# Transposing e by DMA in fours instead of pairs, in the backward pass of grouped-query attention

## The chip, the cores and the metric

The kernel runs on one core of a Trainium2 chip. The metric is the device time of one execution in microseconds (us), and the number of record is the median over runs of the kernel on the chip. A profiled execution is one more run, with its own time. The engines are named PE (TensorE, matmuls), PEld (its weight loads), DVE (VectorE), ACT (ScalarE), POOL (GpSimd) and SP (SyncE, which here only issues DMAs).

## What is computed

The reference is the forward and the backward pass of two attention blocks whose outputs stand side by side. Block A is linear attention; the kernel does it first, before the stage described below, and the change doesn't touch it. Block B, which the change is about, is softmax attention with 16 query heads that share one key and one value head (S = 2048 tokens, D = 448, head size 28):

```
q = x @ wq ; k = x @ wk ; v = x @ wv
p = softmax(q k^T * 28**-0.5) ; o = p v          # per head
B = o (heads side by side) @ wo
outputs: concat([A, B], -1) and the gradients of all eight inputs and weights, given grad_out
```

For the backward pass the kernel needs, for each head, do = grad_out @ wo^T, dV = p^T do, dS = p * (do v^T - rowsum(do * o)), dQ = dS k and dK = dS^T q.

## The kernel before

After block A and the projections of block B, one long stage (from about 229 us on, here called the core) does attention and its gradient together. Its work is cut into 64 **blocks** b of 256 queries x 2 heads (8 query chunks qc, 8 pairs of heads), and each block into 8 **units** of 256 keys; u = 8b + tp counts the 512 units. The loop over u (28 more steps run it dry) is written out by hand under a manual schedule: the order in the source is the order on each engine. In the step of unit u:

- `rows_SD` (L625 by its helper `mmt`) puts the scores of unit u into PSUM banks sps (matmuls with 32 rows of the array), and for unit w = u - 16 the products do v^T into banks dps.
- ACT takes the exponential e of each head's scores into an SBUF slot **eT** (L861 and L899, 128 x 512 each). A slot of eT holds two units (4 KB per partition); ten slots rotate.
- For unit w = u - 16, DVE multiplies dps of one head by e (L866), ACT copies that of the other to SBUF (L868, cp), POOL multiplies it (L869); the results are dsT. DVE transposes dsT in 32 x 32 squares for dK (L931).
- In odd units, when a slot is full, SP issues one DMA that transposes it whole, 128 x 2048 values of 2 bytes, 512 KB, into a slot of **eN** (L902). Twelve slots of 4 KB rotate, and a block has four.
- PE adds e v to oq for the two units before (`o_mm`), dS k for units 18 to 20 back (`dq_mm`), in odd units dK for blocks 27 units behind (`dk_m`), and in even units one **quarter** of dV (`dv_mm`): four matmuls of 512 columns, one per eN slot of the block, in the order c = 0 to 3. dV's quarters of block b are at u = 8b + 18, 20, 22 and 24.
- `due(u, lag)` is the block whose first unit lies lag units back. With it, once per block, DVE copies o^T from oq (lag 9), PE turns it (`onat_T`, lag 10), DVE and POOL normalise it (`o_norm`, lag 10) into the rows do_nat, where it takes the place of do; and so on up to lag 27, where dQ is stored.

Two kinds of work are laid between the units in a spare PSUM bank, at most one per unit: `do_proj`, 32 halves of do for the 16 row tiles (its slots are in the dictionary do_slots), and `out_proj`, the output o @ wo in halves (`out_part` says which half at which unit; four of each query chunk's after it is done, at 64(q+1) + 24 to + 48, and the last two tiles whole at u = 532 and 536). Its left operand, o transposed, is made by an SP transpose of 256 KB after every 8 blocks (L891, into oTq), which stands in the same queue as those of e.

From u = 512 on `post_load` brings grad_out (L711), x (L716) and weights into freed slots of eT and eN through SP's queue, in even units, and from u = 519 `gwo` computes the gradient of wo from them. Then the last stage computes dx, dwk, dwv and dwq.

SP takes its DMAs strictly in order: each waits for its own data, and those behind it wait too.

Of the kernel before, what the change touches and what calls it, by code (L numbers as in the profile page):

```python
# [9 lines left out]
ALU = mybir.AluOpType  # L10
# [14 lines left out]
def kernel(  # L25
# [580 lines left out]
    with ExitStack() as cs_:  # L606
        psA = psc.enter_context(tc.tile_pool(name="psAcc", bufs=1, space=bass.MemoryType.PSUM))
        pe_ = cs_.enter_context(tc.tile_pool(name="ceT", bufs=10, side="right"))
        pn_ = cs_.enter_context(tc.tile_pool(name="ceN", bufs=12, side="right"))
        pd_ = cs_.enter_context(tc.tile_pool(name="cdsT", bufs=5, side="right"))  # L610
# [10 lines left out]

        eT, eN, dsT, dsx, qX, don, doT, rl, prod = ({} for _ in range(9))

# [37 lines left out]
        wo = pp_.tile([P, 4, D], BF16, name="wo", bufs=1)  # L661
        oTq = {}

        def out_part(u):
            n, q_ = (u % 64 - 24) // 8, u // 64 - 1
            if u >= NU and u in (532, 536):
                n = (u - 532) // 4
            elif q_ < 0 or n not in (0, 1, 2, 3) or u % 8 or u >= NU:
                return None
            return (2 * q_ + n, 0, D) if u >= NU else (2 * q_ + n // 2, n % 2 * (D // 2), (n % 2 + 1) * (D // 2))  # L670

        ots = {}

        def out_proj(i, c0, c1, ps):
            for c in range(4):
                mm(ps[:, 0:c1 - c0], oTq[i // 2][:, 4 * (i % 2) + c, :], wo[:, c, c0:c1], start=(c == 0), stop=(c == 3))

# [7 lines left out]
        def by_tokens(t):  # L685
            return t.rearrange("p (t d) -> p t d", d=512)
# [8 lines left out]
        def post_load(k):  # L695
            if k == 4:
                post["dkvT"], mix = (pn_.tile([P, 16, P], BF16, name="eN").rearrange("p a b -> p (a b)") for _ in range(2))
                post["dkvn"], post["wkvT"] = mix[:, 0:1024], mix[:, 1024:1024 + D]
                zero(post["wkvT"][64:128, :])
                nc.sync.dma_start(post["wkvT"][0:64, :], wkvT_d[:, :])  # L700
            if 5 <= k < 9:
                zero(post["dkvT"][64:128, 512 * k - 2560:512 * k - 2048])
            i = k % 4
            rows = slice(i * 512, (i + 1) * 512)
            if k == 8:
                t = pe_.tile([P, 2, 2, 512], BF16, name="eT").rearrange("p a b c -> p (a b c)")
                post["wqT"] = t[:, 0:4 * D].rearrange("p (g c) -> p g c", c=D)
                nc.sync.dma_start(post["wqT"], wqT_d[:, :].rearrange("(g p) c -> p g c", p=P))
            elif k < 4:
                t = by_tokens(pe_.tile([P, 2, 2, 512], BF16, name="eT").rearrange("p a b c -> p (a b c)"))  # L710
                nc.sync.dma_start(t[:, :, 0:D], go2[rows, D:2 * D].rearrange("(t p) d -> p t d", p=P))  # L711
                post["gb"] += [t[:, j, :] for j in range(4)]
            else:
                t = by_tokens(pe_.tile([P, 2, 2, 512], BF16, name="eT").rearrange("p a b c -> p (a b c)"))
                zero(t[:, :, D:512])
                nc.sync.dma_start(t[:, :, 0:D], Bx2[rows, :].rearrange("(t p) d -> p t d", p=P))  # L716
                post["xb"] += [t[:, j, :] for j in range(4)]
# [76 lines left out]
        def o_mm(v):  # L794
            b, tp = divmod(v, 8)
            for t2 in range(2):
                t = 2 * tp + t2
                for h in range(2):
                    mmt(oq[32 * h:32 * h + 32, 0:256], vaug[:, t, :],
                        eT[v // 2][:, v % 2, h, t2 * 256:(t2 + 1) * 256], (0, 32 * h), t == 0, t == 15)  # L800
                yield
# [17 lines left out]
        def dv_mm(b, h, qb):  # L819
            for c in range(4):  # L820
                rhs = eN[4 * b + c][:, :, :].rearrange("p (u h t q) k -> p u h t q k", u=2, h=2,
                                                       t=2)[:, :, h, :, qb, :]
                mmt(dv_acc[32 * c:32 * c + 32, :], don[b][:, qb, h, :], rhs, (0, 32 * c),
                    b == 0 and h + qb == 0, b == NB - 1 and h + qb == 2)
# [5 lines left out]
        def do_copy(i, h, ps):  # L830
            nc.vector.tensor_copy(out=do_nat[:, i, h * 256:(h + 1) * 256], in_=ps[:, 0:256])

        free = [*range(1, 16), *range(17, 27, 2), *range(32, 64, 8),
                *[64 * q_ + i for q_ in range(1, 6) for i in (0, 8, 16, 56)]]
        do_slots = {u: divmod(n, 2) for n, u in enumerate(free[0:2 * NS])}
        with tc.manual_schedule():
            tc.keep_in_program_order(nc.scalar.activation(out=ex[:], in_=ex[:], func=ACT.Exp))
            for u in range(NU + 28):
# [18 lines left out]
                if hasS:  # L857
                    if u % 2 == 0:
                        eT[u // 2] = pe_.tile([P, 2, 2, 512], BF16, name="eT")
                    et = eT[u // 2]  # L860
                    nc.scalar.activation(out=et[:, u % 2, 0, :], in_=sp[0][:, :], func=ACT.Exp, scale=scale)  # L861
                if hasD:
                    dst = pd_.tile([P, 2, 512], BF16, name="dsT")
                    dsT[w] = dst
                    ew = eT[w // 2]
                    nc.vector.tensor_tensor(out=dst[:, 0, :], in0=dp[0][:, :], in1=ew[:, w % 2, 0, :], op=ALU.mult)  # L866
                    cp = pc_.tile([P, 512], BF16, name="cp")
                    nc.scalar.activation(out=cp[:, :], in_=dp[1][:, :], func=ACT.Copy)  # L868
                    nc.gpsimd.tensor_tensor(out=dst[:, 1, :], in0=cp[:, :], in1=ew[:, w % 2, 1, :], op=ALU.mult)  # L869
                for a in {10: (0, 2), 18: (1, 3)}.get(u, ()) or {38: (0, 2), 54: (1, 3)}.get(u % 64, ()) * (u < 448):  # L870
# [15 lines left out]
                if (b := due(u, 10)) is not None:  # L886
                    o_norm(b)
                    if b % 8 == 7:
                        q_ = b // 8
                        oTq[q_] = pp_.tile([P, 8, P], BF16, name="oTq", bufs=1)  # L890
                        nc.sync.dma_start_transpose(oTq[q_][:, :, :], do_nat[:, 2 * q_:2 * q_ + 2, :].rearrange("p q c -> p (q c)"))  # L891
                if (b := due(u, 14)) is not None:
# [5 lines left out]
                if hasS:  # L898
                    nc.scalar.activation(out=et[:, u % 2, 1, :], in_=sp[1][:, :], func=ACT.Exp, scale=scale)  # L899
                    if u % 2 == 1:  # L900
                        en = pn_.tile([P, 16, P], BF16, name="eN")
                        nc.sync.dma_start_transpose(en[:, :, :], et[:, :, :, :].rearrange("p a b c -> p (a b c)"))  # L902
                        eN[u // 2] = en

# [5 lines left out]
                else:  # L910
                    o_dq((u - 2, u - 1), (u - 20, u - 19))
                    b, n = divmod(u - 18, 8)
                    if 0 <= b < NB:
# [121 lines left out]
```

## Time and profile before

| | |
|---|---|
| median of 5 runs | 1106.34 us |
| the runs | 1110.08, 1105.51, 1099.61, 1112.46, 1106.34 us |
| the profiled execution, its own time | 1108.78 us |
| its span (first to last instruction) | 1107.1 us |
| mean granted TensorE clock | 0.994 |
| the core: first exponential L899 to the last one | 229.5 to 1025.8 us |
| first and last dV matmul | 255.1 and 1056.1 us |

The span is counted from the first instruction of the program on the core; all times of the profile are from there. Where a row gives three numbers with slashes they are the least, the median and the greatest duration in ns; "x256" is a count; "out<-in" names what an instruction writes and reads. In brackets stands the idle time of the engine before the instruction and what ended it. In a row of SP, the duration is how long the issue held SP, not how long the transfer took.

### The profile page before, as it was taken

The page shows a single profiled execution, that of the slowest core. Times are in us where ns is not written, and L with a number is a line of the kernel's source. Part 1 is how long each engine was busy: PE and PEld are TensorE (multiplying, and loading weights), DVE is VectorE, ACT ScalarE, POOL GpSimd, SP SyncE. Part 2 cuts the span into 40 slices and gives each one's busy share as a digit, 9 for nine tenths or more (in the row PEclk, how much of TensorE's full clock was granted, in tenths as well). Part 3 has the DMA queues.
Part 4 walks back from the last instruction along what each step waited for, and adds up shares of the span by engine and source line. Part 5 has one row for each costly group of instructions (what it writes and reads, how often), then busy time and mean ns, then how long its engine had stood idle before and what let it go on. Part 6 is the DMA issues. An engine that isn't in the chain of part 4 may idle for free.

```text
span 1107.1 us, 39142 instructions
## 1 busy us (share of the span) xinstructions
PE 1050.2 (95%) x15640; PEld 490.4 (44%) x15645; DVE 897.4 (81%) x1772; ACT 875.9 (79%) x1744; POOL 757.9 (68%) x986
## 2 busy tenths in 40 slices
PE   9999999988999999999999999989999999999998
PEld 5545555444444444444444434434444444444344
DVE  7887400438999999999999999989999999999742
ACT  6453122568999999999999999989999999999421
POOL 6001242227888888889888988978988898888640
PEclk9999999999999999999999999999999999999999
DMA  9869899099999999999999999999999999999962
GB/s 264 149 124 178 174 189 221 27 202 185 203 183 183 187 185 184 181 193 182 190 182 191 192 186 181 189 177 188 191 191 195 182 185 188 195 183 191 218 138 63
DMA packets 672534, 199.01 MB, mean 180 GB/s; under 512 B 649584, under 2 KB 668320, under 8 KB 672352
## 3 DMA queue, kind: packets, MB, share of 16 engines
q1 hardware_dynamic: 660512, 175.19, 99.2%
q0 software_dynamic: 6880, 17.37, 6.5%
q10 hardware_dynamic: 4960, 3.96, 1.2%
q8 instruction: 122, 2.00, 0.7%
q14 instruction: 60, 0.49, 0.1%
HBM read 21.00 MB, written 12.94 MB: 31 GB/s over the span
## 4 chain that ended last, share of the span: by engine, by line
PE 52%; DVE 27%; DMA 7%; ACT 7%; issue 6%; POOL 0%; SPq 0%; DVEq 0%; ACTq 0%
PE agen L80 13%; PE dk_acc L625 11%; DVE dsx L931 10%; DVE dsT L866 9%; DMA eN<-eT 5%; PE sps L80 5%; PE oq L625 5%; ACT eT L899 5%; PE aacc L80 4%; PE sps L625 4%; PE dps L625 4%; PE dv_acc L625 2%; DVE R L884 2%; DVE oTs L881 2%; DVE oTs L754 1%
## 5 line engine op out<-in xcount | busy, mean ns | idle before, releaser
L869 POOL TENSOR_TENSOR dsT<-cp,eT 128x512 bf16<-128x512 bf16 x512 | 588.3, 1155 | 120.0 <-ACT cp L868 108.9
L866 DVE TENSOR_TENSOR dsT<-dps,eT 128x512 bf16<-128x512 f32 x512 | 342.8, 669 | 31.0 <-PE dps L625 23.6
L931 DVE STREAM_TRANSPOSE dsx<-dsT 128x512 f32<-128x512 f32 x512 | 357.5, 698 | 2.0
L861 ACT ACTIVATE eT<-sps 128x512 bf16<-128x512 f32 x512 | 313.0, 611 | 38.2 <-PE dps L625 25.4
L625 PEld LDWEIGHTS <-R 32*128 32x128 bf16 (+1 forms) x8192 | 203.5, 94 | 295.7 <-issue 268.3
L868 ACT ACTIVATE cp<-dps 128x512 bf16<-128x512 f32 x512 | 314.2, 614 | 14.6 <-PE dps L625 13.3
L899 ACT ACTIVATE eT<-sps 128x512 bf16<-128x512 f32 x512 | 320.8, 627 | 0.0
L625 PE MATMUL dk_acc<-dsx,qX 32*32 32x512 bf16 x4096 | 268.8, 377 | 0.0
L625 PE MATMUL dps<-doT,R 32*128 32x256 bf16 x2048 | 249.7, 270 | 12.5 <-DVE dsT L866 7.3
L625 PE MATMUL sps<-R,R 32*128 32x256 bf16 x2048 | 217.8, 274 | 3.7 <-DVE oTs L754 2.0
L625 PE MATMUL oq<-eT,R 128*32 128x256 bf16 x2048 | 158.6, 276 | 0.0
L625 PE MATMUL oq<-dsT,R 128*32 128x256 bf16 x2048 | 158.4, 276 | 0.1
L625 PEld LDWEIGHTS <-qX 32*32 32x32 bf16 x4096 | 79.9, 89 | 114.9 <-issue 54.8
L625 PE MATMUL dv_acc<-eN,don 128*32 128x512 bf16 x1024 | 112.4, 381 | 9.6 <-DMA eN<-eT 9.6
L80 PEld LDWEIGHTS <-R 128*128 128x128 bf16 (+1 forms) x553 | 45.8, 99 | 47.8 <-issue 20.3
L396 POOL MEMSET ga<- 64x448 bf16 x2 | 0.9, 470 | 95.1 <-DVE pr L347 81.8
L546 DVE TENSOR_TENSOR osb<-R 32x512 bf16<-32x512 bf16 x4 | 1.7, 414 | 62.1 <-ACT R L543 62.1
L625 PEld LDWEIGHTS <-don 128*32 128x32 bf16 x1024 | 33.9, 98 | 0.6
L80 PE MATMUL agen<-R,R 128*128 128x448 bf16 x128 | 28.6, 353 | 0.9 <-ACT R L219 0.6
L874 POOL DMA_DIRECT2D qX<-qn_d x32 | 18.1, 570 | 16.2 <-DMA qn_d<-gaT 16.2
L884 DVE TENSOR_SCALAR R<-oq 64x256 bf16<-64x256 f32 x64 | 27.3, 427 | 2.0
L744 PE MATMUL sps<-identF,oTs 64*128 64x64 f32 x128 | 21.4, 247 | 7.4
(220 smaller groups left out, 1010.8 us busy)
## 6 DMA issues: line engine op xcount, KB each, us to landing
qX<-qn_d POOLq DMA_DIRECT2D x32, 256.0 KB, 6.3
eN<-eT SPq DMA_TRANSPOSE x256
out_dram<-osb ACTq DMA_DIRECT2D x22, 112.0 KB
qn_d<-gaT SPq DMA_DIRECT2D x2, 1024.0 KB
xa<-in_A_x_dram SPq DMA_DIRECT2D x8, 224.0 KB
ga<-in_grad_out_dram SPq DMA_DIRECT2D x4, 448.0 KB
xa<-in_grad_out_dram POOLq DMA_DIRECT2D x4, 448.0 KB, 5.7
out_dram<-wdq POOLq DMA_DIRECT2D x8, 224.0 KB, 4.0
```

Of the source, the lines that this page charges most:

```text
L80: nc.tensor.matmul(out_ap, lhsT=lhsT, rhs=rhs, start=start, stop=stop, tile_position=(0, 0))
L625: nc.tensor.matmul(out, lhsT=lhsT, rhs=rhs, start=start, stop=stop, tile_position=pos, skip_group_check=True)
L744: nc.tensor.transpose(onp[:, qb, :, :].rearrange("p h c -> p (h c)"), oTs[0:64, qb * P:(qb + 1) * P], identF[0:64, 0:64], tile_position=(0 ...
L861: nc.scalar.activation(out=et[:, u % 2, 0, :], in_=sp[0][:, :], func=ACT.Exp, scale=scale)
L866: nc.vector.tensor_tensor(out=dst[:, 0, :], in0=dp[0][:, :], in1=ew[:, w % 2, 0, :], op=ALU.mult)
L868: nc.scalar.activation(out=cp[:, :], in_=dp[1][:, :], func=ACT.Copy)
L869: nc.gpsimd.tensor_tensor(out=dst[:, 1, :], in0=cp[:, :], in1=ew[:, w % 2, 1, :], op=ALU.mult)
L874: nc.gpsimd.dma_start(qX[qc][32 * a:32 * a + 32, :, :, :].rearrange("j b s c -> j b (s c)"), qn_d[qc * 256:(qc + 1) * 256, :].rearrange("( ...
L881: nc.vector.tensor_copy(out=oTs[0:64, :], in_=oq[0:64, 0:256])
L884: nc.vector.tensor_scalar(out=qT_B[g][64 * hp:64 * hp + 64, qc * 256:(qc + 1) * 256], in0=oq[64:128, 0:256], scalar1=scale, scalar2=None, ...
L899: nc.scalar.activation(out=et[:, u % 2, 1, :], in_=sp[1][:, :], func=ACT.Exp, scale=scale)
L931: nc.vector.transpose(out=dsx[b][:, tp, :, :, :].rearrange("p h t c -> p (h t c)").bitcast(F32), in_=dsT[y][:, :, :].rearrange("p h c -> p ...
```

## The change

- eT becomes five fixed tiles of four units (8 KB per partition), eN six fixed tiles of 32 x 128 values; both take as much memory as before. `eT(u)` and `eN(b, c)` name the parts. Tiles are no longer taken from a rotating pool, so each reader and writer is ordered by the part of the tile that it touches.
- SP's transpose is issued once per four units, when u % 4 is 3: 128 x 4096 values, 1 MB.
- dV's quarters move two units back: u = 8b + 20, 22, 24 and 26.
- o is transposed after blocks 15, 31 and 47 for two query chunks at once (512 KB), and after 55 and 63 for one; the target is R4, which held the weights of do_proj before. For that, all do_proj slots now lie before u = 128 (the last at 120 instead of 184), and the halves of out_proj lie 16 units apart at 144 to 256 and 272 to 384, and 8 apart at 400 to 456 and 464 to 488.
- The loads after u = 512 go into parts of the same fixed tiles.

The lines of the code shift by a few: L861, L866, L868, L869, L899 and L902 become L865, L870, L872, L873, L903 and L905, and L891 becomes L894.

```diff
-        pe_ = cs_.enter_context(tc.tile_pool(name="ceT", bufs=10, side="right"))
-        pn_ = cs_.enter_context(tc.tile_pool(name="ceN", bufs=12, side="right"))
+        pe_ = cs_.enter_context(tc.tile_pool(name="ceT", bufs=1, side="right"))
+        pn_ = cs_.enter_context(tc.tile_pool(name="ceN", bufs=1, side="right"))
...
+        ETs = [pe_.tile([P, 4, 2, 512], BF16, name=f"eT{i}") for i in range(5)]
+        ENs = [pn_.tile([P, 32, P], BF16, name=f"eN{i}") for i in range(6)]
+
+        def eT(u):
+            return ETs[u // 4 % 5][:, u % 4, :, :]
+
+        def eN(b, c):
+            return ENs[(2 * b + c // 2) % 6][:, 16 * (c % 2):16 * (c % 2) + 16, :]
...
-        oTq = {}
+        oTq = flat(R4).rearrange("p (t k) -> p t k", k=P)
+        outs = {128 * m + 144 + 16 * n: 8 * m + n for m in range(2) for n in range(8)}
+        outs.update({400 + 8 * n: 16 + n for n in range(8)})
+        outs.update({464 + 8 * n: 24 + n for n in range(4)})
...
         def post_load(k):
...
+            t = ETs[(128 + k // 2) % 5][:, 2 * (k % 2):2 * (k % 2) + 2, :, :].rearrange("p a b c -> p (a b c)")
...
-        free = [*range(1, 16), *range(17, 27, 2), *range(32, 64, 8),
-                *[64 * q_ + i for q_ in range(1, 6) for i in (0, 8, 16, 56)]]
-        do_slots = {u: divmod(n, 2) for n, u in enumerate(free[0:2 * NS])}
+        do_slots = {u: divmod(n, 2) for n, u in enumerate([*range(1, 16), *range(17, 27, 2), *range(32, 128, 8)])}
...
-                    if b % 8 == 7:
-                        q_ = b // 8
-                        oTq[q_] = pp_.tile([P, 8, P], BF16, name="oTq", bufs=1)
-                        nc.sync.dma_start_transpose(oTq[q_][:, :, :], do_nat[:, 2 * q_:2 * q_ + 2, :].rearrange("p q c -> p (q c)"))
+                    if b in (15, 31, 47, 55, 63):
+                        t0, t1 = 2 * (b // 8) - 2 * (b < 48), 2 * (b // 8) + 2
+                        nc.sync.dma_start_transpose(oTq[:, 4 * (t0 % 4):4 * (t0 % 4) + 4 * (t1 - t0), :],
+                                                    do_nat[:, t0:t1, :].rearrange("p q c -> p (q c)"))
...
-                    if u % 2 == 1:
-                        en = pn_.tile([P, 16, P], BF16, name="eN")
-                        nc.sync.dma_start_transpose(en[:, :, :], et[:, :, :, :].rearrange("p a b c -> p (a b c)"))
-                        eN[u // 2] = en
+                    if u % 4 == 3:
+                        nc.sync.dma_start_transpose(ENs[u // 4 % 6][:, :, :],
+                                                    ETs[u // 4 % 5][:, :, :, :].rearrange("p a b c -> p (a b c)"))
...
-                    b, n = divmod(u - 18, 8)
+                    b, n = divmod(u - 20, 8)
                     if 0 <= b < NB:
                         dv_mm(b, n // 4, n // 2 % 2)
```

## The prediction

> **What bounds the kernel now.** I read the page first, for where the time lies.
>
> ```profile
> span 1107.1 us, 39142 instructions
> ...
> PE   1050.2 (95%) x15640; PEld 490.4 (44%) x15645; DVE 897.4 (81%) x1772; ACT 875.9 (79%) x1744; POOL 757.9 (68%) x986
> ...
> DMA  9869899099999999999999999999999999999962
> ...
> q1 hardware_dynamic: 660512, 175.19, 99.2%
> ...
> PE 52%; DVE 27%; DMA 7%; ACT 7%; issue 6%; POOL 0%; SPq 0%; DVEq 0%; ACTq 0%
> ```
>
> The stage that the change touches runs from about 229 us (first exponential) to 1056 us (last dV matmul), and its 512 units are nearly all of it. Four engines are at nine tenths or more there, so nothing that shortens one engine's work alone pays much. Beside them stands SP's DMA queue, q1, busy throughout, and the chain passes through a DMA for 7%. So the next view is that of the tile eN: what is issued into it, and who waits for it.
>
> ```profile
> L902 SPq DMA_TRANSPOSE eN<-eT x256: 1334/2982/7247, 235.8 to 1030.0; - x128
> ...
>   DMA eN<-eT: 9.6, 8
> ```
>
> 256 issues in 235.8 to 1030.0 is one per 3.11 us, and an issue holds SP for 2.98 us in the median: SP hardly rests. The waits view books some 700 us of SP's waiting at L902 to ACT, and that is misleading. The timelines show it:
>
> ```profile
> 641.16 0.60 ACT L899 ACTIVATE eT<-sps 128x512 bf16<-128x512 f32 x1
> ```
> ```profile
> 645.43 1.25 SPq L891 DMA_TRANSPOSE oTq<-R  x1
> 646.79 18.51 SPq L902 DMA_TRANSPOSE eN<-eT  x7
> ```
> ```profile
> 652.34 0.42 PE dk_acc L625 x5
> 652.76 6.13 DMA eN<-eT
> 658.89 0.04 issue
> 658.93 0.38 PE dv_acc L625
> ```
>
> The exponential at 641.16 (unit 263) ends at 641.76, and its pair is issued only at 652.76, 11.0 us later, behind earlier pairs. It lands at 658.89, 17.1 us after its data was ready, just too late for dV, whose first quarter reads it 11 units after that exponential: 11 x 1.54 = 16.9 us (a block of 8 units takes 12.33 us by the starts of L899, 12.0 where it has no projection of do or out). Over the run a pair lands 14.6 us after its exponentials in the median and 17.7 in the worst twentieth. Thus the transposes form a queue that is exactly as fast as the engines: 4 x 3.11 = 12.4 us per block, against 12.0 to 12.33. It drifts into the deadline, stops PE, and drifts off. All eight stops lie at the first quarter's fourth chunk, so at one place of the block.
>
> **What a stop costs.** The eight make 9.6 us of idle PE (2.02, 0.50, 0.38, 0.83, 1.42, 0.95, 2.48, 1.05). Refilling costs about 0.3 more each: across the stop of 1.42, L899 starts 3.46 us after the one before, where the same place of undisturbed blocks has 1.70, so 1.76 in all. That is 2.4. And the two longest cost the clock:
>
> ```profile
> 735.49 0.38 PE L625 MATMUL dv_acc<-eN,don 128*32 128x512 bf16 x1 [2.48 <-DMA eN<-eT]
> ```
> ```profile
> 736.15:739.56 3.41, 3.41 (x48) 1.17 (x44) 2.76 (x6) 2.50 (x5) 1.15 (x1) 0.50 0.97 184
> 740.00:750.00 10.00, 9.65 (x186) 4.15 (x178) 9.47 (x19) 9.93 (x21) 8.20 (x9) 1.00 1.20 194
> ```
>
> The columns are the window, its length, each engine's busy time with its count, the granted clock and DMA. 48 matmuls in 3.41 us, where the next stretch does 18.6 per us: (63 - 48) / 18.6 = 0.8 us lost, and by the same count 1.2 at 258.3 to 261.7. Here the row differs from a rule. The Trainium skill ("TensorE: Matmul & The Clock Gate", Part 1) has the clock drop after at least one idle window of about 3.4 us. By it these stops, all under 2.5 us, keep the clock, and eight cost 9.6 + 2.4 = 12.0. By the trace, stops of 2.02 and 2.48 did lose it and one of 1.42 did not, and the cost is 12.0 + 2.0 = 14.0. I take the trace. Adding up instead how much longer the nine disturbed units are gives 13.4; I use that.
>
> **The change, part by part.**
> *Four units per transpose.* It removes 128 of 256 issues; bytes and 256 B packets stay. What an issue costs by itself is read from small ones:
>
> ```profile
> L103 SPq DMA_TRANSPOSE wvT<-R x4: 1192/1242/1356, 26.8 to 30.8; - x4
> ```
> ```profile
> L891 SPq DMA_TRANSPOSE oTq<-R x8: 1247/1250/1420, 345.8 to 1034.3; - x8
> ```
>
> 128 KB take 1.24 us, 256 KB 1.25, 512 KB (eN) 1.33 at the least: a floor of 1.2 us whatever the size. So 128 x 1.2 = 154 us of SP's time go; SP's time is not the path, the stream's is. Upper bound of the gain in the stream: the whole floor, 1.2 us per quad. Lower bound: nothing, since in most of the trace's packets one transpose follows the other with no gap. In the few cycles with no other queue's packet near, packets nearly cease for 0.5 us at the seam of two transposes. Here a rule speaks against the change: the skill ("DMA: Bandwidth & Descriptors", Anatomy of one DMA) says that the fixed part of a DMA is dominated by completion latency, not setup, and with a second transpose already issued that is hidden. By it the gain is 0. The rows of 1.24 us against 1.33 show setup, on the issuing side. I take 0.3 us per quad, nearer to the packets than to the floor: 6.2 - 0.3 = 5.9 us per quad, against 6.0 to 6.17 us in which the engines make one. A loss can't be excluded, as no row has a transpose of 1 MB; I keep 0.3 us the other way as that end.
>
> *dV two units later.* Its first quarter now comes 13 units after its last exponential, 20.0 us instead of 16.9. A quad hands over its first pair 3.1 us later than before; with a queue at work this moves nothing, as the bytes ahead are the same, and without a queue a quad lands after some 1.3 + 2 x 1.9 + 1.5 = 7 us. So 3 us of slack come with it. I set the 256 measured landing-to-landing intervals against block periods free of stops. With no gain in the stream quads still stop PE for some 5 us, since arriving in lumps eats the slack; with 0.25 us per quad no stop is left after the first block; with 0.5 us of loss PE stops in half the blocks.
>
> *Waits.* The exponential of unit 4k+20 now waits for a quad issued after unit 4k+3, 16 units before: 24.7 us, later than dV's 20.0, so dV is hit first. Behind it on ACT stand cp and the other exponential, thus everything, if it were late. POOL's and DVE's reads of the same slot lie four units back, as before three. A quad's own target is freed by dV at unit 8b+26 and the quad comes at 8b+27, as 8b+24 and 8b+25 before: nothing.
>
> *o, out and do.* Eight transposes of 256 KB become three of 512 and two of 256: 3 x 1.25 us of SP, hidden as above. The halves of out_proj (28) and the do_proj slots (32) keep their number and stay one per block at a unit divisible by 8, beside the 0.36 us that each costs a block today (12.33 - 12.0). dV's quarters stay one per even unit. All at nothing; if two fell into one block, 0.36 us each.
>
> *The end.* SP issues the last pair near 1030 and the first load of grad_out after it at 1033.68; PE waits for that load:
>
> ```profile
> 1038.96 0.54 PE L80 MATMUL sps<-eT,R 128*128 128x448 bf16 x2 [1.71 <-DMA eT<-in_grad_out_dram]
> ```
>
> and is at half clock at 1040.0 to 1043.3. With a queue that has drained, the last quad (ready at 1026.4) would be issued by 1027 and leave SP at 1031, so the load comes some 2 us earlier: 1.7 + 1 at best, 0 if the queue is as long as now. I take 1.5.
>
> **Sum**, against the profiled execution's 1108.8 us: 13.4 in the units, less 1 for a stop in the first blocks, where the queue starts 12 us late behind the q transposes, and 1.5 at the end: 1108.8 - 12.4 - 1.5 = 1094.9. The profiled execution lies 2.4 above the median of 1106.3, and stops vary from run to run (1099.6 to 1112.5), while a drained queue has none; so I leave it at **1094.5**, 1.07% under the median. Nothing more can come: the engines' own 12.0 to 12.33 us per block stay.
>
> **Rivals.**
> *The stream gains nothing* (setup is hidden already). For it: packets that abut in most of the trace, q1 at 99%. Then slack and lumps cancel, 5 of the 9.6 us stay, and the time is 1106.3 - 4 = 1102, between 1099 and 1109.
> *A 1 MB transpose is slower than two halves* (slower end). Place: every seam of the queue; the point from which it decides is 6.17 us per quad, today's 2 x 3.11 being at the edge. At 0.3 us over, 128 x 0.3 = 38 us, less the slack of 3, plus clock losses: about 1140. For it: service varies widely already (1.3 to 7.2 us) and no row has the size. Against: same bytes, same packets.
> *The engines are the bound anyway* and stops hide other work: against it, L899's periods lengthen by the full stop each time.
>
> **From cases to numbers.** Drained queue 0.56 (1088 to 1099), no gain 0.28 (1099 to 1109), slower transposes 0.16 (1109 to 1150). A measurement of this kernel tells about 1% from no change, that is 1095.3 to 1117.4. The first case straddles the lower bound: faster 0.44, same 0.43, slower 0.13. The range of 8 in 10 leaves out 0.05 below and 0.14 above: **1088 to 1113**; the likeliest case alone 1088 to 1099.
>
> **What would show it.** Right: eN's 128 issues with a median near 5.5 us, but gaps between them, no wait of dv_acc for eN after the first block, no half-clock window inside the units, blocks still at 12.0 to 12.33 us, the first grad_out load before 1033. No gain: issues back to back at 6.1 us and two to five stops, now at units 8b+20. Wrong: issues over 6.2 us and dv_acc waiting in most blocks, or ACT's exponentials waiting for the eT slot.

## The result, and the profile after

| | before | after |
|---|---|---|
| median of all runs | 1108.89 us (73 runs) | 1097.2 us (38 runs) |
| range | 1096.1 to 1123.3 us | 1094.8 to 1102.7 us |
| ratio, 95% interval | | 0.9918, 0.9903 to 0.9932 |
| profiled execution, its span | 1108.78, 1107.1 us | 1097.16, 1095.4 us |
| first exponential of the core, start | 229.5 us | 230.2 us |
| last one, start | 1025.8 us | 1016.9 us |
| from there to the end of the span | 81.3 us | 78.5 us |

By the ratio the change saves 0.8%; the ratio compares fast runs alone, those within 1.5% of the fastest of their kernel, and so leaves out the longest ones of before, while the medians of all runs lie 1.05% apart. The spread of the runs shrinks from 27 to 8 us. That this is because PE's stops varied from run to run is inferred: each kernel has one profile. The page of the changed kernel first, in the lines that answer to those shown of before:

```profile
span 1095.4 us, 38646 instructions
...
PE 1045.2 (95%) x15640; PEld 490.6 (45%) x15645; DVE 895.9 (82%) x1772; ACT 875.7 (80%) x1744; POOL 757.2 (69%) x986
...
DMA  9879899199999999999999999999999999999962
...
q1 hardware_dynamic: 656320, 175.18, 92.9%
...
PE 34%; POOL 25%; ACT 23%; issue 11%; DVE 4%; DMA 2%; SPq 0%; POOLq 0%; ACTq 0%; DVEq 0%
...
L633 PE MATMUL dv_acc<-eN,don 128*32 128x512 bf16 x1024 | 108.7, 379 | 0.0
```

The engines do the same work as before. What has changed is q1: 92.9% of the span instead of 99.2% for the same 175 MB, so the queue now rests. The idle time ahead of dV's matmuls (the last column, 9.6 us before) is 0.0, and DMA has fallen from 7% to 2% of the chain that ended last. That chain now runs more through POOL and ACT (25% and 23%) than through PE and DVE as before; no run here tests which engine sets the length of a block. The view of the tile eN:

```profile
L905 SPq DMA_TRANSPOSE eN<-eT x128: 4699/5326/7697, 236.4 to 1017.5; - x128
```

The median hold is 5.33 us. From the first issue to the last it is 781 us, 6.15 us from issue to issue, which the engines set now: SP's holds sum to 682 us, and between its DMAs it rests for 93 us in all, where it rested for 28 before. 101 of the 128 quads go out within 0.1 us of the end of their last exponential, where pairs went out 3 to 13 us late. The longest delays follow a 512 KB transpose of o:

```profile
430.99 5.37 SPq L905 DMA_TRANSPOSE eN<-eT  x1
...
437.08 3.10 SPq L894 DMA_TRANSPOSE R<-R  x1
...
440.29 10.51 SPq L905 DMA_TRANSPOSE eN<-eT  x2
```

The timeline puts the quad of 440.29 behind o's 3.10 us; it is 3.4 us late, and the lateness has drained two to three blocks on. In the middle of the core blocks take 11.97 and 12.39 us by turns, like the undisturbed blocks of before.

The start of the core got worse. The timeline of 236 to 249 us after:

```profile
236.36 4.97 SPq L905 DMA_TRANSPOSE eN<-eT  x1
...
241.50 0.46 SPq L580 DMA_DIRECT2D qn_d<-gaT  x1
...
247.45 0.18 DVE L762 RECIPROCAL rl<-sps 128x4 f32<-128x4 f32 x1 [4.69 <-DMA qn_d<-gaT]
247.67 0.29 DVE L763 TENSOR_TENSOR oTs<-sps,rl 128x128 f32<-128x128 f32 x1
...
248.01 0.39 PE L633 MATMUL sps<-R,R 32*128 32x256 bf16 x4 [3.66 <-DVE oTs L763]
```

The same place before, by its chain of waits:

```profile
235.84 2.12 SPq L902
...
238.13 6.11 DMA qn_d<-gaT
```

And the matmul that waited there, by the timeline of before:

```profile
244.93 0.39 PE L625 MATMUL sps<-R,R 32*128 32x256 bf16 x4 [1.19 <-DVE oTs L754]
```

On SP the first transpose of e stands ahead of the second store of q to DRAM (L580). A pair held SP for 2.12 us, a quad for 4.97, so the store goes out at 241.50 instead of 238.13. DVE's reciprocal rl (one over the row sums of the softmax) has nothing to do with q, but its tile was given memory from which that store still reads; so it waits 4.69 us, and PE waits 3.66 us for what DVE makes of it (1.19 before). The granted clock falls to half from 248.6 to 252.0. That it is the memory was read from the kernel here; a run further down moves the tile.

At the other end the first load of grad_out goes out 5.5 us after the start of the last exponential, 7.9 before; PE doesn't wait for it any more, and no window of half clock is left there:

```profile
1005.58 16.68 SPq L905 DMA_TRANSPOSE eN<-eT  x3
...
1022.37 0.55 SPq L720 DMA_DIRECT2D eT<-in_grad_out_dram  x1
```

### The profile page after: what moved, and what is told of

Its sections match the earlier page's. It is cut to its first block, busy times and chain, and to the rows that moved or that the text cites. A ratio compares the mean times of both kernels' runs of the same rounds, so it can differ in the third digit from the quotient of the medians.

```text
span 1095.4 us, 38646 instructions
## 1 busy us (share of the span) xinstructions
PE 1045.2 (95%) x15640; PEld 490.6 (45%) x15645; DVE 895.9 (82%) x1772; ACT 875.7 (80%) x1744; POOL 757.2 (69%) x986
## 3 DMA queue, kind: packets, MB, share of 16 engines
q1 hardware_dynamic: 656320, 175.18, 92.9%
## 4 chain that ended last, share of the span: by engine, by line
PE 34%; POOL 25%; ACT 23%; issue 11%; DVE 4%; DMA 2%; SPq 0%; POOLq 0%; ACTq 0%; DVEq 0%
POOL dsT L873 22%; ACT cp L872 13%; PE agen L80 12%; ACT eT L903 9%; PE aacc L80 4%; PE sps L80 4%; PE oq L633 4%; PE sps L633 2%; PE dv_acc L633 2%; PE dps L80 1%; DVE dsx L934 1%; PE dps L633 1%; PE dk_acc L633 1%; POOL prod L767 1%; POOL don L770 1%
## 5 line engine op out<-in xcount | busy, mean ns | idle before, releaser
L873 POOL TENSOR_TENSOR dsT<-cp,eT 128x512 bf16<-128x512 bf16 x512 | 587.7, 1155 | 105.7 <-ACT cp L872 97.5
L870 DVE TENSOR_TENSOR dsT<-dps,eT 128x512 bf16<-128x512 f32 x512 | 342.4, 669 | 16.3 <-PE dps L633 9.1
L865 ACT ACTIVATE eT<-sps 128x512 bf16<-128x512 f32 x512 | 313.0, 611 | 28.8 <-PE dps L633 12.5
L872 ACT ACTIVATE cp<-dps 128x512 bf16<-128x512 f32 x512 | 315.1, 615 | 11.6 <-PE dps L633 8.0
L903 ACT ACTIVATE eT<-sps 128x512 bf16<-128x512 f32 x512 | 321.6, 628 | 0.0
L633 PE MATMUL dv_acc<-eN,don 128*32 128x512 bf16 x1024 | 108.7, 379 | 0.0
L80 PEld LDWEIGHTS <-R 128*128 128x128 bf16 (+1 forms) x673 | 57.1, 98 | 55.1 <-issue 24.6
L499 ACT ACTIVATE wdq<-agen 128x448 bf16<-128x448 f32 x16 | 8.7, 542 | 25.3 <-PE agen L80 25.3
```

The lines of the kernel that those rows point to most:

```text
L80: nc.tensor.matmul(out_ap, lhsT=lhsT, rhs=rhs, start=start, stop=stop, tile_position=(0, 0))
L633: nc.tensor.matmul(out, lhsT=lhsT, rhs=rhs, start=start, stop=stop, tile_position=pos, skip_group_check=True)
L865: nc.scalar.activation(out=eT(u)[:, 0, :], in_=sp[0][:, :], func=ACT.Exp, scale=scale)
L903: nc.scalar.activation(out=eT(u)[:, 1, :], in_=sp[1][:, :], func=ACT.Exp, scale=scale)
```

## The experiments

My theory was that the size of the transposes does it: fewer issues, a shorter stream, so the queue drains. Rivals: the later deadline of dV does it; or the fixed tiles and the rarer transposes of o. Four kernels take the change apart. Ratios are to the kernel before.

**Quads, but dV at its old place.** The changed kernel with

```diff
-                    b, n = divmod(u - 20, 8)
+                    b, n = divmod(u - 18, 8)
```

> The changed kernel with dV's quarters back at 8b+18 to 8b+24: quads, fixed tiles and the new o transposes stay, the later deadline goes. Issue theory (each transpose costs the queue about 0.9 us beside its bytes, so half as many make the queue faster than the engines and it runs empty): a quad lands some 7 us after its last exponential, far before the 16.4 us at which dV comes, so no wait of dV for eN and the time of the changed kernel, 1096 to 1098 us. Slack theory (the two units are what removes the stops): stops come back, 1102 to 1109 us, with dV waiting for eN in several blocks.

Measured: 1098.16 us, ratio 0.9925 (0.9896 to 0.9954). By its profile no dV matmul waits for eN; eN's row is as after:

```profile
L905 SPq DMA_TRANSPOSE eN<-eT x128: 4709/5258/7664, 235.5 to 1017.1; - x128
```

So the two units of slack aren't needed: a quad that is issued in time, with the queue at rest, lands 6.3 us after its issue in the median.

**Each quad as two halves, issued one after the other.** The changed kernel; bytes, tiles, deadline and unit stay:

```diff
                     if u % 4 == 3:
-                        nc.sync.dma_start_transpose(ENs[u // 4 % 6][:, :, :], ...
+                        for j in range(2):
+                            nc.sync.dma_start_transpose(
+                                ENs[u // 4 % 6][:, 16 * j:16 * j + 16, :],
+                                ETs[u // 4 % 5][:, 2 * j:2 * j + 2, :, :].rearrange("p a b c -> p (a b c)"))
```

> The changed kernel with its 1 MB transpose issued as two of 512 KB one right after the other, at the same unit: same bytes, same moment, same deadline, twice the issues. Issue theory: service of a quad goes from 5.3 back to about 6.2 us, the queue stays full again, issues start many us after their exponentials, and lumps at a full queue stop PE: 1102 to 1112 us. If it is not the number of issues but the lumps, the fixed tiles or the deadline: as the changed kernel, 1096 to 1098 us.

Measured: 1110.05 us, ratio 1.0022 (0.9983 to 1.0060): the whole gain is gone. The rows of eN and of PE's waits:

```profile
L906 SPq DMA_TRANSPOSE eN<-eT x256: 1334/2869/7534, 238.0 to 1032.4; - x128
```
```profile
PE dv_acc L633 <- DMA eN<-eT: 7.5, 6, 3.3
```

SP rests for only 28 us between its DMAs, q1 is at 98.9%, and dV waits 7.5 us in six stops, much as before. Over the 12 runs the spread is back too, 22 us against 6 us of the run before this one. This is the cleanest of the four: nothing but the size of an issue differs.

**Pairs at their old units and dV at its old place, all else changed.**

```diff
-                    if u % 4 == 3:
+                    if u % 2:
+                        j = u // 2 % 2
...
-                    b, n = divmod(u - 20, 8)
+                    b, n = divmod(u - 18, 8)
```

> The changed kernel with pairs of 512 KB issued at every odd unit and dV back at 8b+18, so that of the change only the fixed tiles, the fewer transposes of o and the moved slots of the output and do projections are left. Issue theory: as before the change, 1103 to 1112 us, dV waiting for eN some 6 to 12 us in all. If fixed tiles or o's transposes are what helped: below 1100 us.

Measured: 1107.87 us, ratio 1.0003 (0.9961 to 1.0045), with eight stops again:

```profile
PE dv_acc L633 <- DMA eN<-eT: 7.9, 8, 1.8
```

Fixed tiles, rarer transposes of o and the moved slots are worth nothing that these runs can tell, within about 0.4%.

**The kernel before, with dV two units later** (and each pair issued a unit later, so that the slots of eN suffice; about one unit of slack, 1.5 us, is left of the two).

```diff
-                    if u % 2 == 1:
-                        en = pn_.tile([P, 16, P], BF16, name="eN")
...
-                    b, n = divmod(u - 18, 8)
+                    b, n = divmod(u - 20, 8)
...
+                    if 2 <= u <= NU:
+                        en = pn_.tile([P, 16, P], BF16, name="eN")
```

> The kernel before with dV's quarters two units later, and each pair's transpose issued one unit later (behind dV in the same unit, which its target slot needs), so that about one unit, 1.5 us, of slack is won, or up to two while the queue is behind anyway. Issue theory: a queue as slow as the engines drifts into any fixed deadline, so most stops stay: 1101 to 1108 us. Slack theory: the stops go, 1095 to 1099 us.

Measured: 1108.65 us, ratio 1.0023 (0.9989 to 1.0057).

```profile
PE dv_acc L625 <- DMA eN<-eT: 6.7, 2, 6.5
```

No gain in time: the slack doesn't pay. The profile has two stops instead of eight small ones. The long one, 6.5 us, comes from a single issue that held SP for 9.79 us at 907.70, the longest of the 256 (median 2.90), when pairs already went out some 11.7 us after their exponentials. What made that issue so long wasn't looked into.

**So the size decides. But why?** If an issue had a fixed cost of 0.8 us in the stream, by which pairs and quads differ, single units would pay it once more per pair. The changed kernel with 256 KB for each unit, issued three units after it:

```diff
-                    if u % 4 == 3:
-                        nc.sync.dma_start_transpose(ENs[u // 4 % 6][:, :, :], ...
+                if 0 <= (v := u - 3) < NU:
+                    nc.sync.dma_start_transpose(
+                        ENs[v // 4 % 6][:, 8 * (v % 4):8 * (v % 4) + 8, :],
+                        ETs[v // 4 % 5][:, v % 4, :, :].rearrange("p b c -> p (b c)"))
```

> The changed kernel with one transpose of 256 KB per unit (512 issues), each issued three units after its exponentials so that its target is free. If each issue costs the queue 0.9 us beside its bytes, as 5.3 us for one issue per quad and 6.2 for two say, then four units take 4.4 + 4 x 0.9 = 8.0 us, the queue becomes the bound by far, and the time goes up by 128 x (8.0 - 6.1) = 240 us to some 1340 us. If two halves are only slow for another reason (512 KB just at the engines' pace, with no cost per issue), four quarters cost about what two halves do: 1105 to 1115 us.

Measured, in two runs: 1155.58 us, ratio 1.0457 (1.0362 to 1.0552), far from 1340. The row of eN:

```profile
L916 SPq DMA_TRANSPOSE eN<-eT x512: 1231/1290/7247, 234.2 to 1084.1; - x171
```

512 issues in 849.9 us are 1.66 each, 6.6 us per four units, where pairs take 6.2 and quads 5.3 to 5.4. The constant cost is refuted: doubling the issues from 256 to 512 added 0.4 us per MB, not another 0.8.

**The transposes alone**, in groups of 8 MB by size, with the attention computation left out:

> All of the reference's computation is left out; the outputs are filled with zeros. The kernel only issues transposes of SBUF tiles on SP's queue, each group 8 MB in all, with pieces of 512, 128, 256, 512 KB, 1, 2 MB, 512 KB and 1 MB. With nothing else at work: if an issue costs the queue time that its own setup can't hide, the time per MB falls with the size, 128 KB at 1.3 us a piece (10.4 us per MB), 512 KB at 2.0 us (4.0 per MB), 1 MB at 3.5 us, 2 MB at 6.6 (3.3 per MB). If setup is hidden behind the data, 512 KB, 1 MB and 2 MB take the same time per MB, 3.6 us.

Measured, from the start of one issue to that of the next in the mean, the first of a group left out: 128 KB 1.31 us, 256 KB 1.38, 512 KB 2.52 (the median is 2.4), 1 MB 4.99, 2 MB 9.79. The windows of the five groups, in this order (window, its length, two engines that are idle, clock, DMA share, GB/s):

```profile
81.80:165.90 84.10, 0.00 (x0) 0.00 (x0) 1.00 0.51 102
166.00:210.00 44.00, 0.00 (x0) 0.00 (x0) 1.00 0.98 188
210.10:249.70 39.60, 0.00 (x0) 0.00 (x0) 1.00 1.14 211
249.80:289.40 39.60, 0.00 (x0) 0.00 (x0) 1.00 1.14 212
289.60:328.50 38.90, 0.00 (x0) 0.00 (x0) 1.00 1.15 214
```

Undisturbed, 512 KB and 1 MB run at nearly one rate, 5.0 us per MB, not the 3.6 that I had expected; only below 512 KB does the floor of an issue show. In the kernel the same 512 KB took 3.06 to 3.11 us and 1 MB 5.3 to 5.4. So neither theory holds as stated: the larger size isn't faster, it is disturbed less. What disturbs is to be seen in the packets. Counted over SP's issues in 262 to 1012 us that follow each other without a pause, with a least-squares fit of the period on what other packets start in it (fetches of instructions, q8 and q14 of the page, 8 or 16 KB on one DMA engine; and loads of qX, 256 KB):

| | issues | period with nothing else | one fetch adds | a qX load adds | fetches per issue | mean period |
|---|---|---|---|---|---|---|
| before, 512 KB | 234 | 2.51 us | 0.61 us | 1.26 us | 0.60 | 3.06 us |
| two halves, 512 KB | 232 | 2.46 us | 0.67 us | 1.29 us | 0.59 | 3.03 us |
| after, 1 MB | 15 | 5.04 us | 0.40 us | none there | 0.87 | 5.39 us |

Per MB before: 2 x (2.51 + 0.60 x 0.61 + 0.15 x 1.26) = 6.1 us, with a qX load in 15% of the issues; after: 5.04 + 0.87 x 0.40 = 5.4. The periods with nothing else, 2 x 2.51 and 5.04, are what the transposes take alone, so next to nothing is lost at the seam of two issues. After has few such issues because it has few without a pause, and these 15 aren't quite like the others: they hold no load, which is half of the 0.7 us between the sums, and a fit to so few is rough (counted a little otherwise it gives 0.29 for a fetch). A fit to the holds of all issues in that stretch, paused or not, compares like with like: 242 pairs of before give 2.42 us, 0.60 more per fetch and 1.32 per load; 123 quads of after give 4.97, 0.19 and 0.63. The kernels have about as many loads per MB (0.24 and 0.23) and somewhat fewer fetches after (1.24 and 0.98). So in the kernels a disturbance costs a 1 MB issue half as much as a 512 KB one, or less. But the queue of after is mostly empty and that of before is not, which could matter as much as the size.

**The same, made on purpose.** Three runs, all with the attention computation left out: transposes of both sizes beside a stream of matmuls, beside rows of 16 KB on single DMA engines, and beside instruction streams on four engines with a few loads like qX's.

```diff
+    for i in range(5600):
+        nc.tensor.matmul(ps[i % 4][:, 0:256], ...
...
+    for i in range(60):
+        nc.scalar.dma_start(scr[i % 16:i % 16 + 1, :], big[:, :])
...
+    for i in range(11200): nc.tensor.matmul(...)
+    for i in range(2600): nc.vector.tensor_copy(out=v[:], in_=w[:])
+    for i in range(1300): nc.scalar.activation(out=y[:], in_=w[:], func=ACT.Copy)
```

> The transposes of the stream by themselves once more, in six groups of 8 MB each, alternately 512 KB (16 of them) and 1 MB (8 of them), this time beside a long stream of TensorE matmuls, which brings the fetches of instructions with it; the attention computation is left out and the outputs are zeros. Alone, 512 KB took 2.45 us and 1 MB 4.97 us, the same per MB; in the kernel 512 KB took 3.11 us (6.2 per MB) and 1 MB 5.33 us. Theory 'larger transposes absorb the disturbance of the instruction fetches better': the 512 KB groups cost at least 0.5 us per MB more than the 1 MB groups (say 6.0 against 5.3). Rival 'fetches cost the stream the same time whatever the size': both groups within 0.2 us per MB of each other, at 5.0 to 5.6. Rival 'fetches cost nothing': both at 4.9 to 5.0.

> The same six groups of transposes, alternately 512 KB and 1 MB, with no matmuls but beside 60 small DMAs of 16 KB that each lie on one DMA engine, one about every 4.5 us from ACT's queue; the attention computation is left out and the outputs are zeros. Theory 'a packet that holds one engine for about 1 us stops a transposition until that engine has caught up, and a larger one hides more of this': 512 KB at least 0.3 us per MB dearer than 1 MB, and both above the 4.95 us per MB of the run alone. Rival 'the size has no part in it': both the same per MB within 0.2 us, whether raised or not. If neither is raised here but the 512 KB groups are raised beside the matmuls, what disturbs is not the held engine.

> The transposes of the stream by themselves, in groups of 8 MB of 512 KB, 1 MB and 2 MB by turns (four of 512 KB with the warm-up, four of 1 MB, three of 2 MB), beside streams of plain instructions on TensorE, VectorE, ScalarE and GpSimd, which bring fetches of instructions for all of them, and beside loads of 229 KB from GpSimd's queue like those of qX; the attention computation is left out and the outputs aren't written with results. The kernels' own traces give 2.40 us for a 512 KB issue with no other packets in it and about 4.9 us for 1 MB, the same per MB; a fetch added 0.61 us to a 512 KB issue before, and 0.2 to 0.4 us to a 1 MB issue after; a qX load added 1.26 us and about 0.6 us. Theory 'one and the same disturbance costs the stream less the larger the transposition that it falls into': the 512 KB groups cost at least 0.4 us per MB more than the 1 MB groups at the same number of disturbances, and those of 2 MB less again. Rival 'the cost of a disturbance doesn't depend on the size': all three within 0.2 us per MB once the number of disturbances is allowed for, and the kernels' difference has another cause.

Measured, us per MB (the first issue of a group left out). The last column is what one disturbance added: the group's time less that of as many undisturbed issues (2.52, 4.99, 9.79 us each), by the number of fetches or rows in it:

| beside | 512 KB | 1 MB | 2 MB | added by one, 512 KB / 1 MB / 2 MB |
|---|---|---|---|---|
| matmuls | 5.79, 5.34 | 5.45, 5.49 | | 0.52 / 0.48 |
| 16 KB rows | 5.85, 5.46 | 5.26, 5.38, 5.55 | | 1.02 / 0.57 |
| four engines | 6.12, 5.96, 5.71 | 5.48, 5.49 | 5.26, 5.55 | 0.65 / 0.36 / 0.36 |
| four engines, after their fetches had ended | 5.07 | 5.02 | 4.91 | |

The first two didn't decide by their totals: 0.10 and 0.26 us per MB between the sizes, about the bound of 0.2 that I had set for no difference. Fetches and rows fell unevenly there (a third group of 1 MB beside the matmuls met no fetch and took 4.98); counted by the fetch, the matmuls' run shows no difference (15 and 14 fetches), the rows' run does (9 and 15 rows). The third decided: with 1.2 to 1.6 fetches per MB, 512 KB costs 0.45 us per MB more than 1 MB. In its windows (512 KB, 2 MB, 1 MB, 512 KB; the last column is GB/s) the small size runs at 177, the large ones at 196 to 201:

```profile
255.00:303.70 48.70, 41.21 (x1380) 38.70 (x1373) 45.42 (x97) 46.35 (x75) 41.19 (x97) 0.96 1.20 177
303.90:345.90 42.00, 30.77 (x1032) 28.97 (x1035) 39.16 (x84) 39.97 (x65) 35.50 (x84) 0.96 1.25 201
346.00:389.80 43.80, 34.26 (x1101) 32.25 (x1097) 40.83 (x88) 41.71 (x67) 36.99 (x88) 0.92 1.18 196
390.00:438.00 48.00, 39.02 (x1319) 36.91 (x1313) 44.72 (x97) 45.69 (x74) 40.56 (x96) 0.96 1.21 176
```

That 2 MB would be better still isn't shown. So in two of the three runs, with both sizes in a full queue, one disturbance costs a stream of 512 KB more than one of 1 MB; beside matmuls alone it doesn't. That the larger size is disturbed less is shown, then, but not beside every kind of traffic, and why stays open. In the packets, the stream nearly stops (0 to 4 packets in 0.1 us instead of 83 or more) while the DMA engine that carried a fetch catches up; that a large transpose has more of its own work to fill this with is argued, not shown.

**The start.** The store of q moved from SP's to GpSimd's queue:

```diff
-                nc.sync.dma_start(qn_d[q2, :].rearrange("(t p) c -> p t c", p=P), qn[:, t2, :])
+                [nc.sync, nc.gpsimd][qc // 2].dma_start(qn_d[q2, :].rearrange(...), qn[:, t2, :])
```

> The changed kernel with the second store of q to DRAM (L580) issued from POOL's queue, where nothing else is waiting then, instead of SP's, where it stands behind the first 1 MB transpose of e, which holds SP 4.97 us. If that is what stops PE for 3.66 us at 248 us and costs it the clock, the stop shrinks to under 1 us and the time falls by 3 to 4 us, to 1093 to 1095 us. If the store's own 6 us to land is what counts, 1096 to 1098 us.

Measured: 1100.32 us, ratio 0.9939 (0.9907 to 0.9970), no gain on the change. The store goes out at 239.05, 2.5 us earlier, but lands no sooner beside the first quads, and rl still waits for it. PE stops for 2.73 us instead of 3.66, and half clock then lasts 10.2 us instead of 3.4:

```profile
248.00 0.18 DVE L762 RECIPROCAL rl<-sps 128x4 f32<-128x4 f32 x1 [3.76 <-DMA qn_d<-gaT]
```

So the shared memory was next: rl's pool is opened before that of qX, and no longer covers the source of the store.

```diff
+        pw_ = cs_.enter_context(tc.tile_pool(name="cwk", bufs=4, side="right"))
         pq_ = cs_.enter_context(tc.tile_pool(name="cqX", bufs=2, side="right"))
         pp_ = cs_.enter_context(tc.tile_pool(name="cout", bufs=2, side="right"))
-        pw_ = cs_.enter_context(tc.tile_pool(name="cwk", bufs=4, side="right"))
```

> The changed kernel with one edit: the pool of rl and its neighbours is opened before the pool of the source of q's second store, so that rl no longer lies in memory that this store still reads. Nothing else of the computation, the transposes or their order changes. Theory 'the stop of 3.7 us before the first dv_acc blocks, and the half clock after it, come from the reciprocal waiting for that store': the stop falls to under 1 us, the window of half clock after it goes, and the time falls by 3.7 to 5.5 us, to 1091.5 to 1093.5 us, ratio to the kernel before 0.987. Rival 'the transposes then stop the same unit another way' (the first eN is late, or the store holds something else): PE stops 2 to 4 us at the same place, and the time stays at 1096 to 1098 us, ratio 0.990 to 0.992.

Measured: 1095.45 us, ratio 0.9892 (0.9847 to 0.9938); span 1092.9, 2.5 less than after instead of 3.7 to 5.5. The stop is gone:

```profile
244.66 0.18 DVE L762 RECIPROCAL rl<-sps 128x4 f32<-128x4 f32 x1 [0.69 <-ACT eT L865]
...
247.33 1.16 POOL L878 DMA_DIRECT2D qX<-qn_d  x2 [18.16 <-PE sps L633]
```

Block 2 starts 3.5 us sooner than after, but block 3 only 2.6. PE stops for 1.0 us at don (do divided by the row sums, which POOL makes and PE transposes), as it did for 0.95 us after, and this time a window of half clock comes with it, at 262.8 us. Besides, this execution had half clock for 3.4 us more at 235 to 239, where its instructions are still the same as after. Two windows, after first:

```profile
235.00:237.00 2.00, 2.00 (x24) 1.07 (x24) 0.85 (x2) 1.50 (x4) 0.00 (x0) 1.00 1.20 187
```
```profile
235.00:237.00 2.00, 2.00 (x14) 0.86 (x12) 0.50 (x2) 1.09 (x2) 0.00 (x0) 0.50 1.22 260
```

14 matmuls instead of 24; over 235 to 239 it is 28 against 46, some 1.6 us at 11.5 per us. With it the 2.5 would be 4.1, as expected, but that the next execution would do without it isn't shown. GpSimd's load of qX follows at once when the store has landed, so the store may still have been late for something. The last run adds to this one that the second store of q is issued in unit 3, so that it stands before the first quad on SP:

```diff
+                    if u == 3:
+                        LATE.pop()()
                     if u % 4 == 3:
                         nc.sync.dma_start_transpose(ENs[u // 4 % 6][:, :, :], ...
```

> The kernel of the run before (rl out of the memory of the store's source) with one edit more: on SP's queue the second store of q stands before the first transposition of eN instead of after it. Theory 'what is left of the loss at the start is GpSimd, which waits for that store before it loads qX, and is then late with don': the store goes out about 3 us earlier, GpSimd's wait of 18.2 us shrinks by about 3 us, the stops of 1 us at don go, and the time falls by 0.5 to 2 us against 1095.4 us, to about 1094. Rival 'what is left is the clock, whose half phases come at the start of this stage however it is entered': the store is earlier, and the time stays within 0.5 us of 1095.4.

Measured: 1093.19 us, ratio 0.9875 (0.9823 to 0.9927), span 1091.8. By its timeline the store goes out 3.0 us earlier and qX 3.4:

```profile
238.22 0.36 SPq L581 DMA_DIRECT2D qn_d<-gaT  x1
...
243.90 1.15 POOL L883 DMA_DIRECT2D qX<-qn_d  x2 [14.64 <-PE dps L81]
```

PE still waits 1.0 us at don once, so that part of the theory was wrong; but the window of half clock is gone. That the store took it away isn't shown, since after had that stop at full clock too. The stretch of 262 to 266 us in the run before and in this one (third from the end is the clock):

```profile
262.00:266.00 4.00, 3.46 (x44) 1.51 (x44) 2.55 (x6) 2.52 (x6) 2.95 (x5) 0.60 1.11 201
```
```profile
262.00:266.00 4.00, 3.68 (x67) 1.97 (x68) 3.54 (x8) 3.28 (x7) 3.62 (x5) 1.00 1.24 259
```

44 matmuls against 67. These two versions beat both kernels by their medians, 2 and 4 us under the change; their intervals overlap its own (0.9903 to 0.9932), so the profile, not the ratio, is what speaks for each.

## Why the prediction was right, and where its sum was off

The sum took 13.9 us from the profiled execution (1108.8 to 1094.9); between the two profiled spans it was 11.7 (1107.1 to 1095.4), and the median came to 1097.2 instead of 1094.5. The mechanism was right: a queue that ran just as fast as its users was made faster, drained, and dV's stops went. That the sum came so near owes something to luck: 3.5 us too much in the core and 1.3 too little at the end partly cancel, and the transposes became faster for another reason than the one given. Term by term:

- *The stops of dV and their price, 13.4 us.* Gone, all eight, with the two windows of half clock. Right. What the core shows in net, first to last exponential, is 796.2 to 786.7 us: 9.5 less where the sum had 12.4. It also starts 0.6 us later, so its end comes 8.9 earlier.
- *Loss of 1 us for a stop in the first blocks.* This is the term that was mis-sized: 13.4 - 9.5 = 3.9 us were lost. I looked for a late eN there; what came late was the store of q that stands behind the first quad on SP's queue, and with it DVE's reciprocal, by memory and not by data. From the fourth block on the core gained 11.0 us; its first three blocks took 39.5 us instead of 38.0, although the stop of 2.02 us for eN had gone from them. With the shared memory removed they took 37.0, and with the store ahead of the quad as well 35.8; the spans fell by 2.5 and 3.6. So up to 3.7 of the 3.9 us lie here, by one execution of each, with the clock having its part in it. The row was there to be read: before, PE already waited 1.19 us at this place for the same chain.
- *The end, 1.5 us.* It was 2.8 (81.3 to 78.5): the queue was emptier than assumed, the load of grad_out earlier by 2.4 us against the last exponential, and the whole of stop and half clock went.
- *0.3 us per quad, 5.9 us.* Right in direction, too small: 5.4, a gain of 0.7 to 0.8. And the reason given, setup of an issue that shows in the stream, failed: alone, 512 KB and 1 MB cost 5.04 and 4.98 us per MB. Here the Trainium skill ("DMA: Bandwidth & Descriptors", Anatomy of one DMA) was nearer: the fixed part of a DMA is dominated by completion latency, not by setup. It says so of DMAs that GpSimd issues, not of SP's queue, and it doesn't say that a second transpose hides the fixed part of the first; that step and the gain of 0 were the prediction's own. The step agrees with what the transposes take alone; the gain of 0 didn't follow, because fetches and loads stop the stream, and cost small transposes more in the kernels. The floor of 1.2 us holds, from 1.31 us at 128 KB and 1.38 at 256 KB alone.
- *Nothing for the eT slot, eN's target, o, out and do.* Right: no exponential waits for a slot, and pairs with all those parts gave a ratio of 1.0003.
- *3 us of slack from the later dV.* There, but idle: quads at the old lag gave 0.9925, and pairs with one unit more of slack 1.0023. The landing was put well: a quad in a resting queue lands after 6.3 us, where the estimate was 7.
- *Rivals.* The stream gains something and 1 MB isn't slower than two halves; engines as the bound are refuted by the two halves, which do the same work on them in the old time. (Not all four were at nine tenths in the core before: POOL was at 86%, 430.7 of the 500 us from 400 to 900.) The signs hold: 128 issues at 5.33 us in the median, gaps between them, no wait of dV, no half clock inside the units after the start, the first grad_out load at 1022.

## What to carry to other kernels

Where a queue of DMAs runs just as fast as its users, a few tenths of a microsecond per transfer can decide between no stop and many, and a later deadline, here by one unit, doesn't help: compare the rate of the queue with that of its users block by block. Here larger transfers made it faster; measure whether they do beside the traffic of the kernel, since alone they don't. Before making one larger, list what stands behind it on the same queue and who waits for that, memory that is reused included, because what stands behind the first large transfer moves back by its added length, here 3.4 us.

## What was not expected of the hardware

- Transposes of 512 KB, 1 MB and 2 MB ran at 211 to 214 GB/s alone, and a fetch of 16 KB for an engine's instructions took 0.2 to 0.7 us from the stream: 0.5 to 0.7 in transposes of 512 KB, 0.2 to 0.5 in those of 1 MB.
- Beside four-engine streams, loads of 224 KB from GpSimd's queue, some four in flight, landed after 15.9 us in the median, and a 1 MB transpose then took 22 us. 36 such loads lengthened a group of 8 MB from 40 to 154 us, 3.2 us each, where a qX load in the kernel before added 1.3 to a pair. This wasn't followed up.
- After the start of the core the granted clock fell to half, for 3.4 us or a multiple of it, at most stops of PE of 1.6 us or more and at none of 1.04 to 1.59 us. Length alone didn't decide: in the run of single units half clock came with a stop of 1.61 us and not with ones of 1.71 and 2.46. Nor did the shortest go one way: at don it came with 0.93 to 0.98 us in three runs (at 265.2, 268.7 and 262.8 us), and full clock stayed at 0.95 us after and 0.96 in the last version.
- At 231 us, where the core begins, half clock lasted 3.4 us in three of nine profiles of full kernels (before and after among them), 6.8 in five (the last two versions among them) and 10.2 in one, on the same matmuls. A difference of 1 or 2 us between two profiled executions can be this alone.
